# An attention-plus-MLP block on one core: key groups in the outer loop, all row sums kept on chip, first rows taken tile by tile

## The chip, the cores and the metric

The kernel runs on one core of one Trainium2 chip. The metric is the device time of one execution in microseconds (us); lower is better. TensorE (PE) multiplies matrices into PSUM, its weight loads have a row of their own (PEld); VectorE (DVE), ScalarE (ACT) and GpSimd (POOL) work on tiles of 128 partitions; SyncE (SP) and POOL issue most of the transfers (DMA). "SPq" in a profile is a transfer being issued by SP.

## What is computed

```
mod = (silu(c) @ w_mod) -> sa, ca, ga, sb, cb, gb          # six rows of 512
h = layernorm(x) * (1 + ca) + sa                           # x: 2048 rows x 512
q = h @ wq                                                 # 32 heads of 128; 8 key/value groups, 4 heads each
o = softmax(q k^T / sqrt(128)) v                           # 2048 keys per group
x = x + ga * (o @ wo)
h = layernorm(x) * (1 + cb) + sb
z = gelu(h @ w_in);  z1, z2 = halves of 896                # w_in: 512 x 1792
g = w_sp @ layernorm(z2) + b_sp                            # w_sp: 2048 x 2048, over rows
x = x + gb * ((z1 * g) @ w_out)
```

All inputs and the output are bf16.

## The kernel before, in words

**Tiles.** The 2048 rows are 16 tiles of 128, in four chunks of four tiles (512 rows). A *unit* is one row tile with one key group (four heads): 128 units. A unit has eight *slots*. In slot i, `qk` (L874) makes scores of two key tiles (two matmuls of 512 columns: 4 heads x 128 rows) into one of two PSUM buffers `s_ps` and ACT takes their exponentials into `pT` (L881, 128x1024). `pv` (L898) makes eight matmuls of 129 columns for the unit before: per head, `pT` as weights, values with a column of ones as the moving side, so the softmax sum comes out as column 129. Every fourth slot DVE divides (L909, L910) into `onorm`. After the last slot SP issues a DMA that transposes `onorm` into `oT` (L918), which `wo_proj` (L928) needs as weights; its result is added to the row tile's f32 sum `xacc` (L941), in the last group also scaled, added to `x_sb` and measured for the second layernorm (L946, L947, L673, L674).

**Order of the work.** Chunks are outermost: for each of the four chunks the eight groups are gone through, four units each. So keys `kT` (by a transposing DMA, L689, on SP), values, `wo` (L692, L694, on POOL) and `wq` (L700, on POOL) are loaded 32 times, 512 KB each, and six `xacc` buffers serve. The loop over iterations `it` lays out, slot by slot: `qk(it)`, `pv(it - 1)`, in slots 0 to 3 one matmul of the query projection of the coming group (`qproj`, L815, its copy L823), in slots 4 to 7 one matmul of `wo_proj(it - 2)`. The first layernorm of the next chunk (`ln1_norm` L779 with a transposing DMA L787, `ln1_mod` L795) and the second one (`ln2_norm` L961, DMA L969, `ln2_mod` L975) are hung into slots. The program's order is only a priority: a planner of the language may reorder each engine's instructions.

**Start.** SP issues `c`, four x tiles, the transposed keys of groups 0 and 1 (L689), the rest of x and the MLP's weights; ACT issues `w_mod`; POOL issues `wq`, values and `wo`. The layernorm of all four tiles of chunk 0, the modulation columns (`mod_columns`, L755) and the whole query projection of group 0 come before the first unit, and so do the rows `ga`, `gb` (L842). Then SP is given 32 transposing DMAs for the first half of `w_sp` (`load_wsp`, L649).

**End.** After the last unit come the softmax-sum check (L1030 to L1048, one matmul) and the MLP, in three parts: for each chunk the two halves of `z` (z2: L1065, GELU L1072, its statistics L1077, L1080 and layernorm L1099; z1 transposed: L1085, L1092), with 32 more transposing DMAs for the other half of `w_sp`; then for each 512 output rows seven sums over 16 row tiles (`g_ps`, L1113), the addition of `b_sp` and multiplication by z1 (L1121, L1124), and the projection `o2_ps` (L1134), which DVE finishes (L1142, L1144) and SP writes out (L1145). A branch at the end runs a slower general path when the check's flag is set; on this data it isn't.

`rstd_of` (L659 to L666) is four small POOL operations per layernorm.

Of the kernel before, what the change touches and what calls it, by code (L numbers as in the profile page):

```python
# [15 lines left out]
P = 128  # L16
# [559 lines left out]
def kernel(  # L576
# [39 lines left out]

    x_dram = A_x[0].rearrange("(t p) d -> p t d", p=P)
# [3 lines left out]
    v_dram = A_v_cache[0].rearrange("g (t p) d -> p g t d", p=P)  # L621
    wmod_dram = w_mod.rearrange("(dt p) n -> p dt n", p=P)
# [6 lines left out]
    flag = flagp.tile([1, 1], mybir.dt.int32, name="flag")  # L629
    res = fast.enter_context(tc.tile_pool(name="res", bufs=1))  # L630
    x_sb = res.tile([P, NT, D], BF16, name="x_sb")
# [8 lines left out]
    h2T = res.tile([P, NDT, S], BF16, name="h2T")  # L640
    win_sb = res.tile([P, NDT, F], BF16, name="win_sb")
    wout_sb = res.tile([P, NFT, D], BF16, name="wout_sb")
    bsp_bc = res.tile([P, S], BF16, name="bsp_bc")
    wsp = [None] * NCH
    nc.gpsimd.memset(mhalf[:], -0.5)

    def load_wsp(t):
        for st in range(NT):
            nc.sync.dma_start_transpose(  # L649
                out=wsp[t][:, st, :],  # L650
                in_=B_w_sp[t * 512 : (t + 1) * 512, st * P : (st + 1) * P],
            )

    stat = fast.enter_context(tc.tile_pool(name="stat", bufs=2))

    def rstd_of(mv, n, tag):

        ve = stat.tile([P, CT], FP32, name=f"ve_{tag}")
        nc.gpsimd.tensor_scalar(  # L659
            out=ve[:, :n], in0=mv[:, :, 1], scalar1=LN_EPS, scalar2=None, op0=ALU.add  # L660
        )
        rstd = stat.tile([P, CT], FP32, name=f"rstd_{tag}")
        nc.gpsimd.tensor_tensor(out=rstd[:, :n], in0=ve[:, :n], in1=mhalf[:, :n], op=ALU.pow)
        nmr = stat.tile([P, CT], FP32, name=f"nmr_{tag}")
        nc.gpsimd.tensor_tensor(out=nmr[:, :n], in0=mv[:, :, 0], in1=rstd[:, :n], op=ALU.mult)
        nc.gpsimd.tensor_scalar(  # L666
            out=nmr[:, :n], in0=nmr[:, :n], scalar1=-1.0, scalar2=None, op0=ALU.mult
        )
        return rstd, nmr
# [6 lines left out]
    with tc.tile_pool(name="psum", bufs=1, space=bass.MemoryType.PSUM) as psum, tc.tile_pool(  # L676
        name="kv", bufs=2
    ) as kvp, tc.tile_pool(name="wts", bufs=2) as wts, tc.tile_pool(
        name="acts", bufs=2
    ) as acts, tc.tile_pool(name="small", bufs=3) as small, tc.tile_pool(  # L680
        name="xacc", bufs=6
    ) as xaccp:
        groups = {}

        def load_group(n):

            g = n % HKV
            kT = kvp.tile([P, SK], BF16, name="kT")
            nc.sync.dma_start_transpose(out=kT[:], in_=A_k_cache[0, g])  # L689
            v1 = kvp.tile([P, NKT, DV], BF16, name="v1")  # L690
            nc.gpsimd.memset(v1[:, :, DH:DV], 1.0)  # L691
            nc.gpsimd.dma_start(out=v1[:, :, 0:DH], in_=v_dram[:, g])  # L692
            wo_g = wts.tile([P, REP, D], BF16, name="wo_g")
            nc.gpsimd.dma_start(out=wo_g[:], in_=wo_dram[:, g * REP : (g + 1) * REP, :])  # L694
            groups[n] = dict(kT=kT, v1=v1, wo=wo_g)

        def load_wq(n):
            g = n % HKV
            wq_g = wts.tile([P, NDT, REP * DH], BF16, name="wq_g")
            nc.gpsimd.dma_start(  # L700
                out=wq_g[:], in_=wq_dram[:, :, g * REP * DH : (g + 1) * REP * DH]
            )
            return wq_g

        wqs = {}
        hTs = {}
        qTs = {}

        with tc.tile_pool(name="setup", bufs=1, side="right") as setup:
            wmod_sb = setup.tile([P, NDT, NMOD], BF16, name="wmod_sb")  # L710
            c_bf = setup.tile([P, NDT], BF16, name="c_bf")
            nc.sync.dma_start(out=c_bf[:], in_=c_dram)
            for j in range(CT):
                nc.sync.dma_start(out=x_sb[:, j, :], in_=x_dram[:, j, :])
            nc.scalar.dma_start(out=wmod_sb[:, :, 0 : 2 * D], in_=wmod_dram[:, :, 0 : 2 * D])
            wqs[0] = load_wq(0)
            load_group(0)
            nc.scalar.dma_start(
                out=wmod_sb[:, :, 2 * D : NMOD], in_=wmod_dram[:, :, 2 * D : NMOD]
            )  # L720
            wqs[1] = load_wq(1)
            load_group(1)
            for t in range(1, NCH):
                nc.sync.dma_start(
                    out=x_sb[:, t * CT : (t + 1) * CT, :],
                    in_=x_dram[:, t * CT : (t + 1) * CT, :],
                )
            nc.sync.dma_start(out=win_sb[:], in_=win_dram)
            nc.sync.dma_start(out=wout_sb[:], in_=wout_dram)
            nc.sync.dma_start(out=bsp_bc[:], in_=B_b_sp.partition_broadcast(P))  # L730

            sc = setup.tile([P, NDT], FP32, name="sc")
# [94 lines left out]
            for hh in range(REP):  # L827
                for f in qproj(0, hh):
                    f()
# [354 lines left out]
```

## Time and profile before

| | |
|---|---|
| median of 3 runs | 1531.6 us (1531.58, 1531.60, 1538.72) |
| the profiled execution's own time | 1537.63 us |
| its span, first to last instruction | 1535.8 us |
| PE busy / ACT busy / DVE busy | 1348.6 / 1081.1 / 467.3 us |
| mean granted TensorE clock | 0.968 |
| DMA traffic | 108.99 MB, of which 58.85 MB read from HBM |

The profiled execution lies 1.8 us above its span and 6.0 us above the median. Busy times of PE overlap from one matmul to the next, so pace is read from start to start. In a row of a group stand line, engine, operation, tiles, count, then busy us and mean ns of one; in a timeline row start and length in us, and in brackets the idle time before it and who ended it; in a wait row the total, the number and the longest.

### The profile page before, as it was taken

The page shows a single profiled execution, that of the slowest core. Times are in us where ns is not written, and L with a number is a line of the kernel's source. Part 1 is how long each engine was busy: PE and PEld are TensorE (multiplying, and loading weights), DVE is VectorE, ACT ScalarE, POOL GpSimd, SP SyncE. Part 2 cuts the span into 40 slices and gives each one's busy share as a digit, 9 for nine tenths or more (in the row PEclk, how much of TensorE's full clock was granted, in tenths as well). Part 3 has the DMA queues.
Part 4 walks back from the last instruction along what each step waited for, and adds up shares of the span by engine and source line. Part 5 has one row for each costly group of instructions (what it writes and reads, how often), then busy time and mean ns, then how long its engine had stood idle before and what let it go on. Part 6 is the DMA issues. An engine that isn't in the chain of part 4 may idle for free.

```text
span 1535.8 us, 27625 instructions
## 1 busy us (share of the span) xinstructions
PE 1348.6 (88%) x11955; PEld 875.5 (57%) x12169; DVE 467.3 (30%) x1153; ACT 1081.1 (70%) x1087; POOL 123.7 (8%) x229
## 2 busy tenths in 40 slices
PE   0639999999989989998998999989999998879997
PEld 0326666666656666665666666656666666634443
DVE  2402222222622222224422222234222222364443
ACT  0428887888878878887888888878888888744000
POOL 2100000000200000001100000011100000010000
PEclk9969999999999999999999999999999999989999
DMA  9433333333333323324433323233333332132000
GB/s 300 114 76 70 70 70 66 70 70 70 87 79 70 69 60 72 73 57 80 86 70 70 69 62 70 61 72 80 70 70 70 70 56 39 23 71 53 15 21 23
DMA packets 210002, 108.99 MB, mean 71 GB/s; under 512 B 190928, under 2 KB 195920, under 8 KB 209872
## 3 DMA queue, kind: packets, MB, share of 16 engines
q1 hardware_dynamic: 194992, 53.64, 19.3%
q0 software_dynamic: 13824, 50.34, 12.0%
q10 hardware_dynamic: 1056, 3.15, 0.6%
q8 instruction: 97, 1.59, 0.4%
q14 instruction: 33, 0.27, 0.1%
HBM read 58.85 MB, written 2.10 MB: 40 GB/s over the span
## 4 chain that ended last, share of the span: by engine, by line
PE 66%; DMA 22%; DVE 5%; SPq 4%; issue 1%; ACT 1%; POOL 1%; DVEq 0%; POOLq 0%; ACTq 0%
PE s_ps L874 22%; PE o_ps L898 22%; DMA oT<-onorm 20%; PE misc L928 6%; PE g_ps L1113 6%; PE misc L815 3%; SPq L649 3%; DMA xnT<-xn 2%; PE z_ps L1065 2%; SPq L689 2%; PE z_ps L1085 2%; DVE xacc L941 1%; PE o_ps L1134 1%; DVE onorm L910 1%; DVE bnst L673 1%
## 5 line engine op out<-in xcount | busy, mean ns | idle before, releaser
L881 ACT ACTIVATE pT<-s_ps 128x1024 bf16<-128x1024 f32 x1024 | 1044.6, 1026 | 285.2 <-PE s_ps L874 214.8
L898 PEld LDWEIGHTS <-pT 128*128 128x128 bf16 x8192 | 570.0, 99 | 251.2 <-issue 15.8
L898 PE MATMUL o_ps<-v,pT 128*128 128x129 bf16 x8192 | 657.7, 223 | 0.1
L874 PE MATMUL s_ps<-qT,kT 128*128 128x512 bf16 x2048 | 620.9, 385 | 35.4 <-DMA oT<-onorm 23.8
L909 DVE RECIPROCAL rall<-o_ps 128x2 f32<-128x2 f32 x256 | 43.9, 171 | 857.7 <-PE o_ps L898 857.7
L874 PEld LDWEIGHTS <-kT 128*128 128x128 bf16 x2048 | 199.9, 98 | 124.3 <-issue 8.2
L928 PE MATMUL misc<-wo_g,oT 128*128 128x512 bf16 x406 | 159.4, 394 | 85.9 <-DMA oT<-onorm 85.4
L815 PE MATMUL misc<-hT,wq_g 128*128 128x512 bf16 x420 | 158.6, 386 | 13.3 <-DVE hT L795 13.2
L928 PEld LDWEIGHTS <-oT 128*128 128x128 bf16 x512 | 51.4, 101 | 120.1 <-DMA oT<-onorm 118.9
L910 DVE TENSOR_TENSOR onorm<-o_ps,rall 128x256 bf16<-128x256 f32 x256 | 106.2, 415 | 0.2
L1113 PE MATMUL g_ps<-wsp,z 128*128 128x512 bf16 x440 | 96.9, 379 | 0.4
L823 DVE CAST qT<-misc 128x512 bf16<-128x512 f32 x128 | 88.2, 689 | 9.6 <-PE misc L815 4.8
L941 DVE TENSOR_TENSOR xacc<-misc,xacc 128x512 f32<-128x512 f32 x112 | 77.3, 690 | 4.6
L1113 PEld LDWEIGHTS <-z 128*128 128x128 bf16 x448 | 43.8, 98 | 52.9
L815 PEld LDWEIGHTS <-wq_g 128*128 128x128 bf16 x512 | 50.9, 100 | 17.6 <-issue 17.2
L700 POOL DMA_DIRECT2D wq_g<-in_A_wq_dram x32 | 24.9, 777 | 376.8 <-PE misc L815 215.7
L694 POOL DMA_DIRECT2D wo_g<-in_A_wo_dram x32 | 24.6, 770 | 305.2 <-PE misc L928 198.6
L1121 DVE TENSOR_TENSOR gb<-g_ps,bsp_bc 128x512 bf16<-128x512 f32 x28 | 19.4, 692 | 65.2 <-PE g_ps L1113 65.2
L692 POOL DMA_DIRECT2D v<-in_A_v_cache_dram x32 | 37.5, 1172 | 6.5 <-issue 6.5
L755 PE MATMUL misc<-sc_bf,wmod_sb 128*128 128x1 bf16 x96 | 2.7, 164 | 35.9 <-DVE sc_bf L742 35.9
L691 POOL MEMSET v<- 128x32 bf16 x32 | 4.1, 128 | 358.1 <-issue 246.3
L673 DVE BATCH_NORM_STATS2 bnst<-x_sb 128x6 f32<-128x512 bf16 x32 | 21.7, 689 | 22.9 <-DMA x_sb<-in_A_x_dram 22.4
(61 smaller groups left out, 331.1 us busy)
## 6 DMA issues: line engine op xcount, KB each, us to landing
wq_g<-in_A_wq_dram POOLq DMA_DIRECT2D x32, 512.0 KB, 4.0
v<-in_A_v_cache_dram POOLq DMA_DIRECT2D x32, 512.0 KB, 6.8
wo_g<-in_A_wo_dram POOLq DMA_DIRECT2D x32, 512.0 KB, 4.7
wmod_sb<-in_w_mod_dram ACTq DMA_DIRECT2D x1, 2048.0 KB, 20.2
oT<-onorm SPq DMA_TRANSPOSE x128, 3.8
out_dram<-yout SPq DMA_DIRECT2D x16, 128.0 KB, 1.7
win_sb<-in_B_w_in_dram SPq DMA_DIRECT2D x1, 1792.0 KB, 11.2
x_sb<-in_A_x_dram SPq DMA_DIRECT2D x3, 512.0 KB, 6.2
```

The lines of the kernel that those rows point to most:

```text
L649: nc.sync.dma_start_transpose(out=wsp[t][:, st, :], in_=B_w_sp[t * 512 : (t + 1) * 512, st * P : (st + 1) * P],)
L692: nc.gpsimd.dma_start(out=v1[:, :, 0:DH], in_=v_dram[:, g])
L815: nc.tensor.matmul(q_ps[:], lhsT=wqs[n][:, dt, hh * DH : (hh + 1) * DH], rhs=hTs[ch][:, dt, :], start=(dt == 0), stop=(dt == NDT - 1),)
L823: nc.vector.tensor_copy(out=qTs[n][:, hh, :], in_=q_ps[:])
L874: nc.tensor.matmul(s_ps[:, h * 512 : (h + 1) * 512].rearrange("p (r q) -> p r q", r=REP), lhsT=groups[n]["kT"][:, kt * P : (kt + 1) * P], ...
L881: nc.scalar.activation(out=pTs[u][:, 2 * i : 2 * i + 2, :], in_=s_ps[:].rearrange("p (k q) -> p k q", k=2), func=ACT.Exp, scale=inv_sqrt_dh,)
L898: nc.tensor.matmul(o_ps[:, hh % 2, 0 : DH + 1], lhsT=pTs[u][:, kt, hh * P : (hh + 1) * P], rhs=groups[n]["v1"][:, kt, 0 : DH + 1], start=( ...
L909: nc.vector.reciprocal(out=rall[:, c0 : c0 + 2], in_=o_ps[:, :, DH])
L910: nc.vector.tensor_tensor(out=onorms[u][:, hh - 1 : hh + 1, :], in0=o_ps[:, :, 0:DH], in1=rall[:, c0 : c0 + 2].unsqueeze(2).to_broadcast([ ...
L928: nc.tensor.matmul(X_ps[:], lhsT=oTs[u][:, hh, :], rhs=groups[n]["wo"][:, hh, :], start=(hh == 0), stop=(hh == REP - 1),)
L941: nc.vector.tensor_tensor(out=xaccs[j][:], in0=X_ps[:], in1=xaccs[j][:], op=ALU.add)
L1113: nc.tensor.matmul(g_ps[:], lhsT=z2[:, st, f * P : (f + 1) * P], rhs=wsp[t][:, st, :], start=(st == 0), stop=(st == NT - 1),)
```

## The change

1. **Loops.** Groups are outermost: unit `u` is group `u // 16`, row tile `u % 16`. Each group's four loads are issued once (8 instead of 32 of each), in iterations 4 to 7 of the 16 of the group before. Sixteen `xacc` tiles hold all rows' sums, and all four chunks' `hT` stay in SBUF.
2. **Order.** A manual schedule fixes each engine's order to the program's.
3. **`wo_proj` one unit later**: `it - 3` in place of `it - 2`, three `oT` buffers.
4. **Start.** All loads go out on SP. Keys of group 0 come untransposed (row p of partition p, sixteen keys per partition; values likewise) and are turned by 16 PE transposes, copied by ACT. Row tile 0 is normalised and turned by PE alone, with its own query projection of 128 columns per head; tiles 1 to 3 are turned ahead of the first `qk`, and their projection (384 columns) fills the slots of iteration 0. The other chunks' layernorms stand in iterations 0, 2 and 5 with 16 PE transposes each; the columns for the second layernorm and the rows `ga`, `gb` in iteration 3. The first quarter of `w_sp` is loaded one transposing DMA every six iterations from iteration 21 on.
5. **Layernorm.** `rstd_of` has two POOL operations (add, power) instead of four; DVE subtracts the mean itself.
6. **MLP input beside the last units.** From iteration 128 on, three matmuls of `z` follow each slot (`zrun(3)`): z2 of tiles 0 to 11, then z1 of chunks 0 and 1; z2 of tiles 12 to 15 and z1 of chunks 2 and 3 follow. One GELU covers a whole z2 tile (896 columns) or two chunks of z1 (1024). `w_out` and `b_sp` are loaded then, on POOL; the second and third quarter of `w_sp` on SP after the loop, the fourth after the first quarter has been used.
7. **MLP output.** Each `o2` tile of a quarter is made between the sums of the next one. In the last quarter the sums are split into 384 and 128 columns, and the `o2` of the first three tiles runs beside them; the last tile is finished and written in two halves, by SP and ACT.

The core of the diff:

```diff
+    fast.enter_context(tc.manual_schedule())
+    nc.sync.dma_start(out=k_nat[:].rearrange("p (t d) -> p t d", d=DH), in_=k_rows[:, 0])
...
+    for kt in range(NKT):
+        nc.tensor.transpose(
+            k_ps[:, kt * P : (kt + 1) * P], k_nat[:, kt * P : (kt + 1) * P], ident[:]
+        )
...
-        units = [(n, jj) for n in range(NCH * HKV) for jj in range(CT)]
-        NU = len(units)
+    NU = HKV * NT
...
+    def qk(u, i):
+        g, j = divmod(u, NT)
+        b, jj = g * NCH + j // CT, j % CT
...
+                xaccs[j] = late.tile([P, D], FP32, name=f"xacc{j}", bufs=1)
...
+    rest0 = qproj(0, list(range(REP)), P, 512 - P)
+    at(0, 0, lambda: ln1_turn(1, CT - 1, xns0))
+    for i in range(NSLOT):
+        fill[0, i] = rest0[2 * i : 2 * i + 2]
+    ln1_at(0, 1)
+    ln1_at(2, 2)
+    ln1_at(5, 3)
+    at(3, 0, mod_rest)
...
+    for st in range(NT):
+        at(21 + 6 * st, 2, lambda st=st: load_wsp(wsp[0], 0, st))
+    for g in range(1, HKV):
+        it = (g - 1) * NT + 4
+        at(it, 3, lambda g=g: load_k(g))
+        at(it + 1, 3, lambda g=g: load_v(g, v_dram, nc.gpsimd))
+        at(it + 2, 3, lambda g=g: load_wo(g, nc.gpsimd))
+        at(it + 3, 3, lambda g=g: load_wq(g, nc.gpsimd))
...
+    for it in range(NU + 6):
...
-            wf = wo_proj(it - 2) if it >= 2 and it - 2 < NU else []
+        wf = wo_proj(it - 3) if 3 <= it < NU + 3 else []
+        for i in range(NSLOT):
+            for fn in later.pop((it, i), []):
+                fn()
             if it < NU:
+                qk(it, i)
+            if 1 <= it <= NU:
+                pv(it - 1, i)
+            for fn in fill.pop((it, i), []):
                 fn()
+            if i >= 4 and wf:
+                wf[i - 4]()
+            if it >= NU:
+                zrun(3)
```

`set_fill(b)` spreads the 16 matmuls of the next block's query projection over slots 0 to 3 of four iterations, as before; `at(it, slot, fn)` hangs a step into a slot.

## The prediction on record

> **What bounds the kernel now.** I read the page first, to see which engine sets the pace; then ACT's timeline, whose exponentials are the clockwork of the 128 units; then PE's waits inside the long stretch of units, and the granted clock by stage.
>
> ```profile
> span 1535.8 us, 27625 instructions
> PE 1348.6 (88%) x11955; PEld 875.5 (57%) x12169; DVE 467.3 (30%) x1153; ACT 1081.1 (70%) x1087; POOL 123.7 (8%) x229
> ...
> L881 ACT ACTIVATE pT<-s_ps 128x1024 bf16<-128x1024 f32 x1024 | 1044.6, 1026 | 285.2 <-PE s_ps L874 214.8
> ```
>
> PE is the fullest engine and ACT waits for it. The timeline gives the pace of both:
>
> ```profile
> 60.46 19.36 ACT L881 ACTIVATE pT<-s_ps 128x1024 bf16<-128x1024 f32 x21 [53.74 <-PE s_ps L874]
> 106.20 1.02 ACT L881 ACTIVATE pT<-s_ps 128x1024 bf16<-128x1024 f32 x1 [26.39 <-PE s_ps L874]
> ...
> 111.83 8.78 ACT L881 ACTIVATE pT<-s_ps 128x1024 bf16<-128x1024 f32 x8 [0.31 <-PE s_ps L874]
> ...
> 620.36 8.77 ACT L881 ACTIVATE pT<-s_ps 128x1024 bf16<-128x1024 f32 x8
> 629.28 8.77 ACT L881 ACTIVATE pT<-s_ps 128x1024 bf16<-128x1024 f32 x8
> ...
> 1328.60 7.91 ACT L881 ACTIVATE pT<-s_ps 128x1024 bf16<-128x1024 f32 x8
> ```
>
> Two unhindered units start 629.28 - 620.36 = 8.92 us apart: 1.115 us a slot. ACT alone could do a slot in (19.36 - 1.03) / 20 = 0.917 us, as its first 21 exponentials show. So an unhindered unit is PE's, and 8.92 us is its price. The units' real rate is worse: 24 exponentials lie ahead of 111.83, so unit 3 starts there, and unit 127 at 1328.60. That is 1216.8 us for 124 units, 9.81 each. Why:
>
> ```profile
> PE misc L928 <- DMA oT<-onorm: 54.5, 39, 4.2
> PE s_ps L874 <- DMA oT<-onorm: 23.8, 12, 3.0
> PE s_ps L874 <- ACT pT L881: 1.8, 5, 0.9
> ...
> 80.00:106.00 26.00, 1.30 (x4) 0.48 (x5) 0.00 (x0) 0.00 (x0) 0.00 (x0) 0.56 0.43 96
> 106.00:112.00 6.00, 5.78 (x41) 3.99 (x41) 0.83 (x3) 3.25 (x4) 0.00 (x0) 0.61 0.00 0
> 112.00:1328.00 1216.00, 1125.77 (x10701) 764.98 (x10893) 337.26 (x865) 1013.81 (x992) 98.38 (x167) 0.98 0.33 68
> 1337.00:1355.00 18.00, 5.49 (x57) 3.45 (x54) 13.73 (x37) 0.00 (x0) 3.92 (x12) 0.76 0.15 31
> 1355.00:1407.00 52.00, 51.31 (x242) 24.62 (x246) 29.66 (x70) 35.03 (x61) 6.81 (x16) 0.95 0.41 84
> 1407.00:1528.00 121.00, 120.14 (x546) 53.97 (x555) 52.26 (x87) 0.00 (x0) 0.00 (x0) 1.00 0.05 16
> ```
>
> The waits are PE's between 112 and 1328 us: 78.3 us on the transposed `oT`, next to nothing on ACT. The windows (columns: PE, PEld, DVE, ACT, POOL, clock, DMA share, GB/s) add that the granted clock is 0.98 there, some 0.02 x 1216 = 24 us more, and where it is below 1 PE had just stood idle (80 to 112, 1337 to 1355). [...] The 24 us are not added to the difference below, which holds them already.
>
> **The change part by part.** Six pieces of the span, each before and after.
>
> *First exponential.* The start before:
>
> ```profile
> 3.65 23.00 SPq L689 DMA_TRANSPOSE kT<-in_A_k_cache_dram  x2
> 6.31 0.17 DVE L734 CAST c_f<-c_bf 128x4 f32<-128x4 bf16 x1 [5.31 <-DMA c_bf<-in_c_dram]
> 32.13 1.29 DVE L673 BATCH_NORM_STATS2 bnst<-x_sb 128x6 f32<-128x512 bf16 x2 [9.91 <-DMA x_sb<-in_A_x_dram]
> 50.14 6.53 PE L815 MATMUL misc<-hT,wq_g 128*128 128x512 bf16 x16 [13.25 <-DVE hT L795]
> ...
> 60.07 42.06 SPq L649 DMA_TRANSPOSE wsp<-in_B_w_sp_dram  x32
> ...
> 0.00:40.00 40.00, 0.99 (x32) 1.03 (x33) 11.07 (x39) 1.49 (x2) 8.67 (x19) 1.00 0.97 302
> ...
> L673 DVE BATCH_NORM_STATS2 bnst<-x_sb 128x6 f32<-128x512 bf16 x32 | 21.7, 689 | 22.9 <-DMA x_sb<-in_A_x_dram 22.4
> L663 POOL TENSOR_TENSOR rstd_ln<-ve_ln,mhalf 128x4 f32<-128x4 f32 x4 | 4.1, 1029 | 9.5 <-DVE xn L779 9.5
> L961 DVE TENSOR_SCALAR xn<-x_sb,rstd_ln,nmr_ln 128x512 bf16<-128x512 bf16 x16 | 6.6, 413 | 24.3 <-POOL nmr_ln L666 24.3
> ```
>
> SP's 23 us on the transposed keys and DVE's wait for x go. Afterwards what the first `qk` needs ends with x tiles 1 to 3, behind `c`, tile 0, 1 MB of `w_mod` and 512 KB of keys: 2.05 MB, 6.8 us at the 302 GB/s of the first 40 us. Counted from the queue's start that is 8 us, from `c`'s landing near 6 it is 13; I take 10. Then three statistics (3 x 0.69, and 0.2 each for the aggregation, 2.7), POOL's power (1.03 and 0.5 around it), three `xn` (1.2), twelve PE transposes at half clock (no such row; by a 129-column `pv` matmul, 0.055 us warm, 0.11 cold, 1.4; by the cold 512-column one of L815, 0.41, it would be 4.9; the width decides for the first) and a `qk`, 0.6: first exponential near 18, with queueing among the small steps 20, between 17 and 27. Before 60.46: **-40.5**.
>
> *Units 0 to 2.* Before 111.83 - 60.46 = 51.4 us: PE stood 26.39 us for the first `oT`, queued behind 42 us of `w_sp` transposes on SP. Those are now one every six units. After: 8 slots at ACT's 0.917, two units at 8.92, 25.2; DVE has about 9 us of work in iteration 0 (the next chunk's four statistics and `xn`, 5.1, and eight PSUM copies at some half us, an estimate) against 7.3 us, and PE needs that `hT` next: +3 (0 to 6). **-23.2.**
>
> *Units 3 to 126.* The pace of a 512-column matmul is read from an undisturbed run of them, less the last one's 0.38:
>
> ```profile
> 1476.53 10.74 PE g_ps L1113 x49
> ```
>
> ```profile
> L910 DVE TENSOR_TENSOR onorm<-o_ps,rall 128x256 bf16<-128x256 f32 x256 | 106.2, 415 | 0.2
> ```
>
> so (10.74 - 0.38) / 48 = 0.216 us. Before 1216.8. After 120 units at 8.92 (1070.4), and four without projection (iterations 3, 124, 125, 126) at 8.92 - 4 x 0.216 = 8.06 (32.2): 1102.6, **-114.2** if the late `oT` is gone. Is it?
>
> ```profile
> DMA to landing us min/median/max: 2.4/3.8/8.1
> ```
>
> `onorm` is done some 0.6 us after the last `pv` slot (0.415 of it is the row above, the rest the reciprocal ahead of it); `wo_proj` needs `oT` in slot 4 of the next iteration but one of the `pv`: four slots and 0.9 us on, so 4.8 us against a median of 3.8 and a maximum of 8.1 from issue to landing. One unit more makes 13.7 us: covers the worst, with 5 us for SP's queue. What is next late is nothing in the row of PE's waits but ACT's 1.8 us. DVE's queue: `onorm`, the `qT` copy and `xacc` are the same per unit. SP's queue: behind each `load_k` stands an `oT` 4.5 us later, and one `w_sp` transpose comes every six units.
>
> Added on PE: 48 transposes of later tiles (0.055 each, 2.6), and `mod_rest`, which leaves the start: 32 one-column matmuls (0.99 in the 0:40 row) and eight of 512 columns (1.7). **+5.3.** Three of four group loads go, off the path; worth nothing by themselves.
>
> *Last exponential to the last z matmul.*
>
> ```profile
> 1355.64 8.33 PE z_ps L1065 x32
> ...
> 1370.01 6.05 PE z_ps L1065 x32
> ...
> 1406.30 4.96 PE g_ps L1113 x23
> ```
>
> Before: unit 127's exponentials end at 1336.5, the first z matmul starts at 1355.64 and cold (8.33 against 6.05), and the first row sum starts at 1406.30: 69.8 us. After: z itself, 128 x 6.05 / 32 = 24.2 and 112 x 0.216 = 24.2; 64 `pv` matmuls, 3.6; twelve of `wo`, 2.6: 54.6 of PE work without a gap. The cover of the layernorm chain is now z2 of tiles 0 to 11, and DVE becomes the narrow one:
>
> ```profile
> L1077 DVE BATCH_NORM_STATS2 stz<-z 128x6 f32<-128x448 bf16 x32 | 19.2, 611 | 9.9 <-ACT z L1072 8.3
> L1099 DVE TENSOR_SCALAR z<-z,rstd_lnz,nmr_lnz 128x896 bf16<-128x896 bf16 x16 | 7.1, 508 | 8.3 <-POOL nmr_lnz L666 8.3
> L975 DVE TENSOR_SCALAR h2T<-xnT,modc 128x128 bf16<-128x128 bf16 x64 | 16.7, 331 | 31.3 <-DMA xnT<-xn 31.3
> L674 DVE BATCH_NORM_AGGREGATE mv<-bnst 128x2 f32<-128x6 f32 x32 | 5.3, 176 | 0.5
> ```
>
> Until tile 15's `h2T`: twelve z2 statistics (twice 0.61 and an aggregation, 17), twelve z2 layernorms (6.1) and about 5 waiting for POOL's power, three row tiles finished by three passes and a statistics one of 0.69 and an aggregation (8.8), four `xn` (1.6), five `h2T` (6.6), the last unit's division (1.2): 46.5 us, while PE comes to z2 of tile 15 after some 41. Stall +3 (0 to 8). 57.6; **-12.2.**
>
> *Sums over rows and output.*
>
> ```profile
> 1358.64 43.09 SPq L649 DMA_TRANSPOSE wsp<-in_B_w_sp_dram  x32
> ...
> 1521.33 6.40 PE L1134 MATMUL o_ps<-wout_sb,yT 128*128 128x512 bf16 x27
> ...
> 1529.91 0.69 DVE L1144 TENSOR_TENSOR yout<-tmp,x_sb 128x512 bf16<-128x512 f32 x1 [1.44 <-DMA out_dram<-yout]
> ```
>
> 560 matmuls at 0.216 are 120.9 us of the 121.5 there; splitting columns 384 + 128 keeps their number of columns. Gain at most 0.6. The fourth quarter's 16 transposes (43.09 / 32 = 1.35 each, 21.6 us) now stand ahead of the first output transfers on SP; with two `yout` buffers DVE stands at the third tile from about 15 to 23 us into that quarter, and PE's two PSUM banks cover 8.5: +0 to 3, taken as 0.6. After the last matmul (1527.7) came 8.1 us; half tiles on two queues spare one pass, and the wait on `yout`: **-2.**
>
> *Sum.* 1535.8 - 40.5 - 23.2 - 114.2 + 5.3 - 12.2 - 2 = **1349** us of span, 1351 of device time. The profiled execution stood 6.0 above the median of the runs shown; I can't tell from which rows, and take off half: **1348**.
>
> **The rivals.** *The tail of queues is longer* (DVE in the z stage, SP in the output, start late): every bound at its upper end, 7 + 3 + 5 + 2.4, or one FIFO order that I misread, gives 1365 to 1388. For: DVE, 29.66 us busy in the 52 us of the old z stage, becomes nearly full, as the layernorms and sums of the last rows join it. Against: each piece has cover. 0.13.
>
> *`oT` stays late where loads share SP:* seven key loads, 16 `w_sp` transposes and sixteen layernorm ones, at 3 to 4 us with the clock's price: +75 to +155, 1425 to 1500. Against: 13.7 us of slack and 8.1 at worst. 0.04.
>
> *PE without pauses gets less clock; slower than before.* [...] The PE-bound part is 1102 + 55 + 121 = 1278 us; it decides below a clock of 0.87, where they grow by 184, and at the 0.76 of the 1337:1355 row they would grow by 404: 1752. Against: 1.00 in the 1407:1528 row, PE 120.14 of 121 us busy. 0.02. [...]
>
> *The fixed order puts a new wait into each unit.* `pv` needs the previous unit's last exponential in slot 1, whose end is at 620.36 + 8.77 = 629.13 in the rows above, while that `pv` follows a `qk` whose own exponential starts near 629.28 + 1.115 = 630.4: 1.2 us to spare. A wait of over 184 / 128 = 1.44 us in all units would make it slower than before. Against: the old slots show the same sequence and 1.8 us of such waits in all. 0.03 near 1550, a third of that within 0.5% of the old time.
>
> *It doesn't do what it says:* the extra unit of slack only pays if the planner had not already moved `wo_proj` as late; the waits of 78.3 us on `oT` show that it hadn't. Then only start and drain would gain, 1348 + 114 = 1462. 0.01 beside the case of the late `oT`.
>
> **How the numbers follow.** Forecast 0.77, with its own range 1332 to 1364 (start -3 to +7, DVE -3 to +5, units' first stage -3 to +3, the half of 6 us either way). The queue case reaches 1388; 1332 to 1388 holds some 0.88 by these chances, and I keep its width because one reading of a queue carries the upper part. Measurement tells about 0.5% (8 us). Faster 0.95, same 0.01, slower 0.04.
>
> **What would show it.** Right: first exponential at 17 to 27 us; unit starts 8.92 apart with hardly a wait on `oT`; clock at 1.00 from 25 us on; HBM reads down by 24 x 2 MB = 48 of 58.85 MB; no PE gap above 3 us before the sums; some waits of z2's matmuls on `h2T`. Wrong: PE waiting for `oT` near key loads; exponentials waited for in slot 1; DVE rows between last `pv` and z2 of tile 12 with PE idle above 8 us; a clock under 1 in the units.

## The result, and the profile after

| | us | ratio to before, 95% interval |
|---|---|---|
| before, median of 4 runs beside the changed kernel | 1533.41 (1531.58 to 1538.72) | 1 |
| the changed kernel, median of 4 runs | 1362.37 (1362.17 to 1363.74) | 0.8881 [0.8857, 0.8906] |
| forecast | 1348, range 1332 to 1388 | |

The time fell by 11.2% and lies in the range, 14.4 us above the forecast. The page of the changed kernel first: span, engines, traffic, and the group of exponentials that the prediction started from.

```profile
span 1360.8 us, 27642 instructions
PE 1318.9 (97%) x12137; PEld 873.7 (64%) x12345; DVE 476.7 (35%) x1171; ACT 1079.6 (79%) x1059; POOL 45.5 (3%) x88
...
HBM read 21.63 MB, written 2.10 MB: 17 GB/s over the span
...
L886 ACT ACTIVATE pT<-s_ps 128x1024 bf16<-128x1024 f32 x1024 | 1046.0, 1024 | 106.5 <-PE s_ps L879 30.3
```

PE's share went from 88% to 97%; ACT's exponentials cost what they did, but stand idle for 106.5 us instead of 285.2. ACT's timeline gives the stages:

```profile
17.11 1.02 ACT L886 ACTIVATE pT<-s_ps 128x1024 bf16<-128x1024 f32 x1 [4.60 <-PE s_ps L879]
...
28.50 8.83 ACT L886 ACTIVATE pT<-s_ps 128x1024 bf16<-128x1024 f32 x8 [0.70 <-PE s_ps L879]
...
51.87 7.91 ACT L886 ACTIVATE pT<-s_ps 128x1024 bf16<-128x1024 f32 x8 [3.46 <-PE s_ps L879]
59.93 8.77 ACT L886 ACTIVATE pT<-s_ps 128x1024 bf16<-128x1024 f32 x8 [0.15 <-PE s_ps L879]
68.85 7.66 ACT L886 ACTIVATE pT<-s_ps 128x1024 bf16<-128x1024 f32 x7
...
1157.09 7.91 ACT L886 ACTIVATE pT<-s_ps 128x1024 bf16<-128x1024 f32 x8
...
1198.60 1.94 ACT L1108 ACTIVATE z1T<-s_ps 128x1024 bf16<-128x1024 f32 x2 [8.53 <-DVE x_sb L952]
```

Units 4 and 5 start 68.85 - 59.93 = 8.92 us apart, the price of an unhindered unit in the prediction. Unit 3 starts at 51.87 and unit 127 at 1157.09. The last row does not belong to the units: it is the next to be read. PE's longest waits say the same from the other side:

```profile
PE o_ps L759 <- DMA wmod_a<-in_w_mod_dram: 7.3, 1, 7.3
PE s_ps L1100 <- ACT z1T L1108: 7.1, 1, 7.1
PE misc L796 <- DVE hT L803: 3.3, 3, 1.1
PE misc L1205 <- DVE gb L1214: 1.4, 1, 1.4
PE misc L796 <- DVE xn L679: 1.1, 1, 1.1
PE s_ps L1220 <- DVE tmp L1235: 1.1, 1, 1.1
```

No wait on `oT` is left. The first row lies in the start; the second is a wait that the kernel before did not have. By stage (PE, PEld, DVE, ACT, POOL, clock, DMA share, GB/s):

```profile
28.50:1157.10 1128.60, 1115.65 (x10960) 767.71 (x11147) 351.02 (x887) 1030.37 (x1009) 30.82 (x54) 1.00 0.16 32
1165.00:1229.30 64.30, 56.93 (x306) 28.55 (x309) 47.99 (x118) 29.16 (x31) 9.92 (x18) 0.92 0.32 74
1229.30:1353.60 124.30, 120.82 (x659) 60.93 (x670) 53.12 (x100) 1.02 (x1) 0.00 (x0) 1.00 0.20 47
```

In the units the clock is 1.00 and the DMA share half of the 0.33 before. It is the middle stage, the rest of `z`, that falls behind: PE is idle for 7.4 of its 64.3 us, at a clock of 0.92. The first row sum starts at 1229.13. So, between the same points of both traces (us):

| stage | before | after | difference | forecast |
|---|---|---|---|---|
| start to first exponential | 60.46 | 17.11 | -43.4 | -40.5 |
| to unit 3 | 51.4 | 34.8 | -16.6 | -18.7 |
| unit 3 to unit 127 | 1216.8 | 1105.2 | -111.6 | -113.3 |
| unit 127 to the first row sum | 77.7 | 72.0 | -5.7 | -12.2 |
| row sums to the end | 129.5 | 131.7 | +2.2 | -2 |
| span | 1535.8 | 1360.8 | -175.0 | -186.7 |

(The forecast's +5.3 is spread here as it falls: 0.9 each for the transposes of iterations 0, 2 and 5, 2.7 for the rows in iteration 3, ahead of unit 3.)

### The profile page after: what moved, and what is told of

It reads as the page before. It is cut to its first block, busy times and chain, and to the rows that moved or that the text cites. A ratio compares the mean times of both kernels' runs of the same rounds, so it can differ in the third digit from the quotient of the medians.

```text
span 1360.8 us, 27642 instructions
## 1 busy us (share of the span) xinstructions
PE 1318.9 (97%) x12137; PEld 873.7 (64%) x12345; DVE 476.7 (35%) x1171; ACT 1079.6 (79%) x1059; POOL 45.5 (3%) x88
## 3 DMA queue, kind: packets, MB, share of 16 engines
HBM read 21.63 MB, written 2.10 MB: 17 GB/s over the span
## 4 chain that ended last, share of the span: by engine, by line
PE 93%; DVE 3%; SPq 2%; issue 1%; DMA 1%; POOL 0%; ACT 0%; ACTq 0%; POOLq 0%; DVEq 0%
PE o_ps L901 35%; PE s_ps L879 35%; PE misc L843 7%; PE misc L933 6%; PE misc L1205 6%; PE s_ps L1100 2%; SPq L1012 1%; PE o_ps L1220 1%; PE s_ps L1064 1%; DMA wq_g<-in_A_wq_dram 1%; DVE stz L1081 1%; PE misc L796 0%; PE s_ps L1220 0%; DVE hT L803 0%; DVE z L679 0%
## 5 line engine op out<-in xcount | busy, mean ns | idle before, releaser
L886 ACT ACTIVATE pT<-s_ps 128x1024 bf16<-128x1024 f32 x1024 | 1046.0, 1024 | 106.5 <-PE s_ps L879 30.3
L843 PE MATMUL misc<-hT,wq_g 128*128 128x512 bf16 (+2 forms) x462 | 169.1, 376 | 0.8 <-DMA wq_g<-in_A_wq_dram 0.8
L933 PE MATMUL misc<-wo_g,oT 128*128 128x512 bf16 x386 | 145.7, 377 | 0.0
L1205 PE MATMUL misc<-wsp,z 128*128 128x512 bf16 (+2 forms) x555 | 100.5, 336 | 1.9 <-DVE gb L1214 1.4
L852 DVE CAST qT<-misc 128x512 bf16<-128x512 f32 (+1 forms) x129 | 87.3, 676 | 1.7 <-PE misc L843 1.7
L1214 DVE TENSOR_TENSOR gb<-misc,bsp_bc 128x512 bf16<-128x512 f32 (+2 forms) x35 | 20.4, 584 | 60.9 <-PE misc L1205 60.9
L1100 PE MATMUL s_ps<-hT,win_sb 128*128 128x512 bf16 x109 | 27.2, 408 | 7.3 <-ACT z1T L1108 7.1
L1108 ACT ACTIVATE z1T<-s_ps 128x1024 bf16<-128x1024 f32 x14 | 14.2, 1024 | 20.1 <-PE s_ps L1100 11.6
L1064 PE MATMUL s_ps<-win_sb,hT 128*128 128x448 bf16 x128 | 27.0, 352 | 0.1
L1074 ACT ACTIVATE z<-s_ps 128x896 bf16<-128x896 f32 x16 | 14.7, 917 | 15.0 <-PE s_ps L1064 15.0
L1100 PEld LDWEIGHTS <-win_sb 128*128 128x128 bf16 x112 | 11.6, 103 | 22.5 <-issue 11.0
## 6 DMA issues: line engine op xcount, KB each, us to landing
win_sb<-in_B_w_in_dram SPq DMA_DIRECT2D x1, 1792.0 KB, 13.7
```

Source lines behind the costliest of these rows:

```text
L843: nc.tensor.matmul(ps[0][:, o0 : o0 + n], lhsT=wqs[g][:, dt, hh * DH : (hh + 1) * DH], rhs=hTs[ch][:, dt, c0 : c0 + n], start=(dt == 0), s ...
L852: nc.vector.tensor_copy(out=qTs[b][:, hs[0] : hs[-1] + 1, c0 : c0 + n], in_=ps[0][:, 0 : len(hs) * n].rearrange("p (h q) -> p h q", q=n),)
L886: nc.scalar.activation(out=pTs[u][:, 2 * i : 2 * i + 2, :], in_=s_ps[:].rearrange("p (k q) -> p k q", k=2), func=ACT.Exp, scale=inv_sqrt_dh,)
L933: nc.tensor.matmul(X_ps[:], lhsT=oTs[u][:, hh, :], rhs=groups[g]["wo"][:, hh, :], start=(hh == 0), stop=(hh == REP - 1),)
L1064: nc.tensor.matmul(ps[0][:, hf * 512 : hf * 512 + FC], lhsT=h2Ts[j // CT][:, dt, (j % CT) * P : (j % CT + 1) * P], rhs=win_sb[:, dt, FH + ...
L1100: nc.tensor.matmul(ps[0][:, k * 512 : (k + 1) * 512], lhsT=win_sb[:, dt, f * P : (f + 1) * P], rhs=h2Ts[2 * ch2 + k][:, dt, :], start=(dt ...
```

## The experiments

Eleven kernels, in three batches, each with runs of the kernel before on the same chip (medians 1536.1, 1535.9 and 1534.8). None leaves out work. Times are compared with the changed kernel's 1362.37 directly where the difference is well above the spread of the runs.

**Is it the unit of slack, or the traffic that is gone?** The largest term, the late `oT`, has two possible causes for its end: `wo_proj` stands one unit later (theory A), or three quarters of the loads no longer stand beside the transfers (rival B). Two kernels do one without the other.

*The old loop order with only `wo_proj` (and the second layernorm) one unit later:*

```diff
-        for it in range(NU + 3):
+        for it in range(NU + 4):
...
-            if it >= 2 and it - 2 < NU:
-                wn, wjj = units[it - 2]
+            if it >= 3 and it - 3 < NU:
+                wn, wjj = units[it - 3]
...
-            wf = wo_proj(it - 2) if it >= 2 and it - 2 < NU else []
+            wf = wo_proj(it - 3) if it >= 3 and it - 3 < NU else []
```

> The kernel before with one edit: wo_proj and the second layernorm behind it take unit it - 3 in place of it - 2, so oT has 13.7 us instead of 4.8 us before PE needs it. Theory A (the slack is what the 114 us between units 3 and 126 were short of): the waits of PE on oT between 112 and 1328 us fall from 78 us to under 15, units start 8.9 to 9.1 us apart there, the time falls by 90 to 115 us to 1420 to 1445. Rival B (oT is late because SP and the 16 DMA engines are full of the 32-fold group loads, and lateness just grows with the queue): the waits stay above 45 us and the time falls by less than 40 us.

Measured 1428.44 us (1427.79 to 1430.97), ratio 0.9294 [0.9253, 0.9336]. PE's waits, without those ahead of the first unit:

```profile
PE misc L928 <- DMA oT<-onorm: 22.6, 2, 18.7
...
PE f_ps L1047 <- DVE bad L1041: 11.4, 1, 11.4
PE o_ps L898 <- DVE onorm L910: 6.2, 5, 2.8
```

What `oT` takes from issue to landing, in the view of that tile, and then the stage of the units in the windows:

```profile
DMA to landing us min/median/max: 2.4/4.0/8.1
```

```profile
112.00:1217.00 1105.00, 1098.81 (x10810) 748.29 (x10808) 334.53 (x859) 1004.73 (x984) 97.14 (x166) 1.00 0.37 74
```

Of what is left on `oT`, 18.7 us lie at the start, behind the `w_sp` transposes, and 3.9 behind the last unit; between 112 and 1217 us PE is busy for 1098.8 of 1105.0. Landing is as slow as it was (median 4.0, maximum 8.1; 3.8 and 8.1 before), so nothing arrives earlier: it is only asked for later. Theory A holds: one unit of slack, in four lines, is worth 1536.1 - 1428.4 = 107.7 us by itself, of 171.0 for the whole change.

*The new kernel with `wo_proj` at its old distance* (from iteration 9 on; iteration 8 does two units):

```diff
-        wf = wo_proj(it - 3) if 3 <= it < NU + 3 else []
+        if it < 8:
+            wf = wo_proj(it - 3) if it >= 3 else []
+        elif it == 8:
+            wf = wo_proj(5) + wo_proj(6)
+        else:
+            wf = wo_proj(it - 2) if it < NU + 2 else []
```

> The changed kernel with wo_proj at it - 2 again (from unit 7 on; units 5 and 6 share iteration 8, the layernorm behind it moves with it). Theory A (slack alone took the waits away): with 4.8 us oT is late again, 60 to 110 us more, 1420 to 1470. Rival B (traffic alone): oT now lands in a median of 2.4 us instead of 3.8, which fits into 4.8; only the ones next to the seven key loads, the 16 w_sp transposes and the last layernorms are late, some 30 times up to 3 us: 0 to 30 us more, 1360 to 1392. If e1 falls as A says and this one stays as B says, either of the two changes would have done alone.

Measured 1369.80 us (1368.97 to 1371.72), ratio 0.8917 [0.8877, 0.8957]. PE's first wait, the landing of `oT`, and ACT's unit 127:

```profile
PE misc L933 <- DMA oT<-onorm: 14.4, 13, 2.0
```

```profile
DMA to landing us min/median/max: 2.4/2.4/6.8
```

```profile
1174.18 7.91 ACT L886 ACTIVATE pT<-s_ps 128x1024 bf16<-128x1024 f32 x8 [0.15 <-PE s_ps L879]
```

Landing has a median of 2.4 us with the loads gone, and 13 waits of at most 2.0 us are all that comes back. Unit 127 starts 17.1 us later than in the changed kernel; as the last sums come one unit earlier and the 7.1 us wait on `z1T` is gone, some 10 are given back and 7.4 remain. So rival B holds as well: the new order with its fewer loads, at the old distance, leaves 14.4 of the old 78.3 us of waits; the slack alone leaves none from unit 4 to the last. The two are not additive; the change pays twice for most of this term. Which part of the new order does it is not separated here: besides the group loads that are gone, SP no longer has the burst of `w_sp` transposes ahead of the units, nor the transposing DMAs of the first layernorm.

**What is the new 7 us wait?** After the units DVE ends a row sum late, ACT's first z1 GELU waits for it, and PE for ACT, though z1 has no use for the second layernorm of tile 15. The timelines of DVE, then PE, of the changed kernel:

```profile
1194.53 1.78 DVE L679 TENSOR_SCALAR z<-z,mvz,rstd_lnz 128x896 bf16<-128x896 bf16 x4 [1.48 <-POOL rstd_lnz L675]
1196.23 0.69 DVE L946 TENSOR_TENSOR xacc<-misc,xacc 128x512 f32<-128x512 f32 x1
...
1197.67 0.69 DVE L952 TENSOR_TENSOR x_sb<-xacc,x_sb 128x512 bf16<-128x512 f32 x1
...
1199.67 11.48 PE L1100 MATMUL s_ps<-hT,win_sb 128*128 128x512 bf16 x39 [7.11 <-ACT z1T L1108]
```

ACT starts at 1198.60, 0.24 us after L952 has ended. L952 is the last reader of the row sums `xacc`, and `z1T` is laid into the memory that their pool leaves (theory A); DVE is late there because z2 layernorms and their wait for POOL stand ahead of it. The rival is that ACT or PE itself was late.

*z2's first three layernorms after the last row sums:*

```diff
-            zq[-1] = [zq[-1], lambda ch=j // CT: z2_norm(ch)]
+            pass
...
+    for ch in range(3):
+        z2_norm(ch)
```

> The changed kernel with the layernorms of z2 of chunks 0 to 2 issued after the last z1 tile of chunks 0 and 1 instead of between the z2 tiles: the same work, later in DVE's queue. Theory A (ACT's first z1 GELU waits 8.5 us for the last row sum on DVE because z1T lies in the memory that the row sums leave, and DVE gets there late since two rounds of z2 layernorms of 1.8 us and their 1.5 us waits for POOL stand ahead): DVE comes there some 6.5 us earlier, PE's 7.1 us stall on s_ps falls below 1.5 us, the time falls by 5 to 7 us to 1355 to 1358. Rival B (DVE's sum of work is the bound): the same work only moves, PE waits for h2T at tiles 12 to 15 or the row sums wait for z2, and the time stays within 2 us.

Measured 1353.29 us (1353.11 to 1353.44), ratio 0.8807 [0.8768, 0.8846], 9.1 us less than the changed kernel. DVE's and ACT's timeline, PE's wait, and the stage's window:

```profile
1190.94 0.69 DVE L952 TENSOR_TENSOR x_sb<-xacc,x_sb 128x512 bf16<-128x512 f32 x1
...
1191.87 1.94 ACT L1108 ACTIVATE z1T<-s_ps 128x1024 bf16<-128x1024 f32 x2 [1.90 <-DVE x_sb L952]
```

```profile
PE s_ps L1100 <- ACT z1T L1108: 0.5, 1, 0.5
```

```profile
1165.00:1220.00 55.00, 54.52 (x310) 27.97 (x309) 47.19 (x117) 29.15 (x31) 11.38 (x18) 1.00 0.34 81
```

The row sum ends 6.7 us earlier, ACT follows it as before, and PE's wait is 0.5. The gain is larger than the wait, as the clock of that stage goes from 0.92 to 1.00 too. PE's 54.5 us between 1165 and 1220 are the "54.6 us of PE work without a gap" of the prediction.

*The first half of the first three z1 tiles in memory beside z2 instead:*

```diff
+            zs["z1a"] = z2p.tile([P, 3, 1024], BF16, name="z1a")
...
-            zs["z1T"] = mlp.tile([P, NFT, S], BF16, name="z1T")
+            zs["z1b"] = mlp.tile([P, NFT - 3, 1024], BF16, name="z1b")
+            zs["z1c"] = mlp.tile([P, NFT, 1024], BF16, name="z1c")
```

> The changed kernel, DVE's order untouched, but the first half of the first three z1 tiles lies in memory beside z2 and not in that of the row sums; the other four z1 tiles stay where they were. Theory A (the 7.1 us stall is a wait for memory: ACT's first GELU of z1 waits until DVE has used the last row sum, nothing in the data asks for it): three GELUs go ahead, PE's wait on s_ps falls from 7.1 to 1 to 3 us, the time falls by 4 to 6 us to 1356 to 1358. Rival B (DVE's amount of work bounds the stage, the memory only names the place): PE stands as long a few tiles later, on h2T or on the sums' z2, the time stays within 2 us of 1362.

Measured 1356.73 us (1356.50 to 1356.94), ratio 0.8832 [0.8797, 0.8866]. ACT's timeline, then PE's waits:

```profile
1191.17 1.02 ACT L1113 ACTIVATE z1a<-s_ps 128x1024 bf16<-128x1024 f32 x1 [0.81 <-PE s_ps L1105]
...
1198.90 1.94 ACT L1113 ACTIVATE z1b<-s_ps 128x1024 bf16<-128x1024 f32 x2 [3.25 <-DVE x_sb L952]
```

```profile
PE s_ps L1105 <- ACT z1b L1113: 1.9, 1, 1.9
...
PE s_ps L1064 <- DVE hT L977: 1.3, 1, 1.3
```

DVE's order is as in the changed kernel, yet the tiles in their own memory are written 7.4 us sooner; the first that lies in the row sums' memory, `z1b`, still waits for L952. That shows the memory as the cause. The last row is the wait on the second layernorm's columns that the prediction had named for this place. In the changed kernel it doesn't show; with the planner, below, it stands beside the other one.

**Does the fixed order matter?**

*The changed kernel with the planner:*

```diff
-    fast.enter_context(tc.manual_schedule())
```

> The changed kernel without the manual schedule, so that the planner orders each engine again. Theory A (the fixed order is worth nothing in the units, whose slots look the same before and after, and a little at start and end): units still 8.92 us apart, the time within -5 and +15 us of 1362. Rival B (the planner's order was part of the lost 114 us): waits of over 30 us on oT or on exponentials appear, 1395 or more.

Measured 1371.17 us (1370.02 to 1372.59), ratio 0.8926 [0.8887, 0.8966]. PE's waits (line numbers are one lower here), then ACT's unit 127:

```profile
PE s_ps L1099 <- ACT z1T L1107: 8.1, 1, 8.1
...
PE s_ps L1063 <- DVE hT L976: 4.0, 1, 4.0
```

```profile
1157.53 7.91 ACT L885 ACTIVATE pT<-s_ps 128x1024 bf16<-128x1024 f32 x8 [0.15 <-PE s_ps L878]
```

Unit 127 starts 0.4 us later than with the fixed order: the units gain nothing by it. Almost all of the 8.8 us comes after that, where DVE is narrow. The start holds a lesson of its own: here the first exponential came at 22.79 us, 5.7 later than in the changed kernel, and yet unit 3 started at 52.18, only 0.3 later. An early first exponential is worth little by itself as long as PE has the same work to do up to unit 3.

*The old loop order with later `wo_proj`, and the `w_sp` transposes spread* (written into iterations 8, 11, 14 and so on, in place of one burst ahead of the units):

```diff
-            load_wsp(t)
...
+        for k in range(2 * NT):
+            at(8 + 3 * k, 2, lambda k=k: nc.sync.dma_start_transpose(
+                out=wsp[k // NT][:, k % NT, :],
...
```

> The kernel of e1 (before with the later wo_proj), and the 32 w_sp transposes that SP issued in one go ahead of the first units now one every three iterations from iteration 8 on. Theory A (the first units stand for oT behind that burst alone): the 18.7 us wait of e1 goes, unit 4 starts some 19 to 24 us sooner than its 112.0 us, the time falls from 1428 to 1404 to 1410, and no new wait on oT appears. Rival B (the first units wait for something else as well, the burst only shows): unit 4 starts less than 10 us sooner, 1418 or more.

Measured 1427.72 us (1425.02 to 1431.47), ratio 0.9288 [0.9251, 0.9325]: no change. SP's timeline says why, and PE's wait on `oT` is the old one:

```profile
60.11 42.10 SPq L989 DMA_TRANSPOSE wsp<-in_B_w_sp_dram  x31
```

```profile
PE misc L926 <- DMA oT<-onorm: 21.4, 2, 17.5
```

The planner issued 31 of the 32 at once, as soon as SP was free. The run tells nothing about the burst; it shows that written order is only a priority there.

*The same with the fixed order:*

```diff
+    fast.enter_context(tc.manual_schedule())
```

> The kernel of e5 with a manual schedule, so that each engine keeps the program's order; e5 had shown that the planner pulls the w_sp transposes back to the front (31 of the 32 issued from 60 to 102 us again), so the burst was never moved. Theory A (the burst is what the first units wait for; moving it takes a fixed order): the 17.5 us wait of PE on oT goes, unit 4 starts near 95 us or earlier instead of 112, the time falls from 1428 to 1400 to 1412. Rival B (the start is slow for another reason, or the program's order makes new waits in the old loop): 1420 or more.

Measured 1415.75 us (1415.49 to 1416.39), ratio 0.9231 [0.9195, 0.9266]. ACT's timeline, then one of PE's waits:

```profile
57.33 32.16 ACT L880 ACTIVATE pT<-s_ps 128x1024 bf16<-128x1024 f32 x32 [50.70 <-PE s_ps L873]
89.64 8.77 ACT L880 ACTIVATE pT<-s_ps 128x1024 bf16<-128x1024 f32 x8 [0.15 <-PE s_ps L873]
```

```profile
PE f_ps L1051 <- DVE ones_c L1049: 15.7, 1, 15.7
```

Now the transposes are spread, and the first 32 exponentials run through: unit 4 starts at 89.64, 22.4 us earlier than the 112.01 of the kernel with only the later `wo_proj`. 2.7 of these are an earlier first exponential (57.33 instead of 60.04); the other 19.7 are the stall behind the burst. Theory A holds for the stall, but the time lies between the two ranges, as only 12 to 13 us reach the median: 3.2 are lost in the units, where PE now waits 8.1 us for `wq_g`, and 3.7 behind them, where it waits 15.7 us for the flag's matmul instead of 11.4; and the profile that is compared with lies 2.5 above its kernel's median. So the fixed order is what makes spreading possible, and it must be written right at every place.

*The changed kernel with the 16 transposes of the first quarter of `w_sp` in one burst, in iteration 21:*

```diff
-        at(21 + 6 * st, 2, lambda st=st: load_wsp(wsp[0], 0, st))
+        at(21, 2, lambda st=st: load_wsp(wsp[0], 0, st))
```

> The changed kernel with the 16 transposes of the first w_sp quarter issued together in iteration 21 instead of one every six iterations: 16 x 1.31 = 21 us of SP. Theory A (oT has 13.7 us and lands in 2.4, so a burst costs only what goes beyond 11.3 us): the oT behind it comes some 10 us late, one stall of 7 to 12 us with 1 to 2 us for the clock, 1370 to 1376. Rival B (the transfers themselves are too little to matter, SP's queue lets oT through): within 3 us of 1362.

Measured 1368.31 us (1366.89 to 1369.81), ratio 0.8907 [0.8872, 0.8943], 5.9 us more. The timeline of SP and of ACT, PE's wait, and the window around it:

```profile
215.10 22.35 SPq L1012 DMA_TRANSPOSE wsp<-in_B_w_sp_dram  x16
...
241.82 1.02 ACT L886 ACTIVATE pT<-s_ps 128x1024 bf16<-128x1024 f32 x1 [4.69 <-PE s_ps L879]
243.97 1.02 ACT L886 ACTIVATE pT<-s_ps 128x1024 bf16<-128x1024 f32 x1 [1.12 <-PE s_ps L879]
```

```profile
PE misc L933 <- DMA oT<-onorm: 4.2, 1, 4.2
```

```profile
241.00:246.00 5.00, 5.00 (x35) 3.31 (x34) 0.10 (x1) 2.62 (x3) 0.00 (x0) 0.66 0.12 22
```

SP issues for 22.35 us without a break, an `oT` stands behind it, and the unit of slack covers all but 4.2 us. Then two exponentials start 2.15 us apart instead of 1.115, at a clock of 0.66: the rest of the 5.9. The mechanism is the expected one, but the time lies between the two ranges: the `oT` that PE waited for became ready at 222.70, 7.6 us into the burst, and was issued at 237.96. Of these 15.3 us the slack of 11.3 covers all but 4.0; the expectation had it ready when the burst began.

**The start and the tail.**

*Keys of group 0 by a transposing DMA, at the same place of SP's queue:*

```diff
-    nc.sync.dma_start(out=k_nat[:].rearrange("p (t d) -> p t d", d=DH), in_=k_rows[:, 0])
+    nc.sync.dma_start_transpose(out=kT0[:], in_=A_k_cache[0, 0])
...
-    for kt in range(NKT):
-        nc.tensor.transpose(
...
```

> The changed kernel with the keys of group 0 loaded by one transposing DMA, as before, in the place of the plain load (no PE transposes, no ACT copies, keys and values of group 0 in their usual order). Theory A (the transposing load is slow while the start's loads fill the DMA engines: 18 us of issue in the trace before, and SP issues x tiles 1 to 3 behind it): first exponential at 28 to 37 us instead of 17.1, the time 11 to 20 us longer, 1373 to 1382. Rival B (in a queue of its own place it lands as it does in the units, 4.4 us after issue): first exponential before 21 us, 1359 to 1366.

Measured 1363.52 us (1363.16 to 1364.23), ratio 0.8890 [0.8856, 0.8925]. SP's and ACT's timeline:

```profile
2.25 4.74 SPq L699 DMA_TRANSPOSE kT<-in_A_k_cache_dram  x1
...
18.27 1.02 ACT L875 ACTIVATE pT<-s_ps 128x1024 bf16<-128x1024 f32 x1 [14.32 <-PE s_ps L868]
```

The transposing load keeps SP for 4.74 us here, and the first exponential comes 1.2 us later. In the kernel before, the first of the two such loads took 18.33 us and the second 4.62; together they are the 23.00 us (start, length):

```profile
3.65 18.33 SPq L689
22.03 4.62 SPq L689
```

My theory, that the transposing load is what held the start, falls; the rival holds.

*The last quarter's sums not split into 384 and 128 columns:*

```diff
-        spatial(last, yT, f, 0, n_a)
+        spatial(last, yT, f, 0, 512)
...
-    for f in range(NFT):
-        spatial(last, yT, f, n_a, P)
...
```

> The changed kernel with the last quarter's sums in 512 columns as in the other quarters, o2 of all four last tiles beside them and finished one after the other at the end. Theory A (the split pays by keeping DVE's finishing of three tiles off the end): the end grows by three tiles of 1.4 us, less the 1.7 us that PE waits inside the split part: 1363 to 1366. Rival B (the split only costs: short matmuls and DVE's extra small passes): 1358 to 1361.

Measured 1363.15 us (1362.89 to 1363.50), ratio 0.8887 [0.8853, 0.8921]. The 0.8 us are within the spread of the changed kernel's own runs (1362.17 to 1363.74): undecided, and at most worth a microsecond.

**A version that beats both.** The kernel with the later z2 layernorms, and besides: the layernorm of the early iterations one slot earlier with its two halves of transposes in two slots, and all outputs issued by ACT, away from SP's transposes.

```diff
-        at(it, 5, lambda: st.update(x=ln1_norm(ch * CT, CT, st["r"])))
-        at(it, 7, lambda: ln1_turn(ch * CT, CT, st["x"]))
+        at(it, 4, lambda: st.update(x=ln1_norm(ch * CT, CT, st["r"])))
+        at(it, 6, lambda: ln1_turn(ch * CT, CT, st["x"], (0,)))
+        at(it, 7, lambda: ln1_turn(ch * CT, CT, st["x"], (1,)))
...
-            (nc.sync if k == 0 else nc.scalar).dma_start(out=out_dram[:, j, s], in_=yout[:, s])
+            nc.scalar.dma_start(out=out_dram[:, j, s], in_=yout[:, s])
```

> The kernel of e3 and two more edits: the 16 PE transposes of each later chunk are laid into two slots (eight each, the layernorm one slot earlier), and all output transfers are issued by ACT, so that they don't stand behind the 16 transposes of the last w_sp quarter. Theory A: PE no longer waits 3.3 us for hT between the halves, DVE no longer stands 7.8 us for an output transfer and PE's 1.4 us there goes: 1353.3 falls by 4 to 6 us to 1347 to 1350. Rival B (these waits are covered by the next matmuls' slack or ACT's queue adds as much): 1352 or more.

Measured 1350.86 us (1350.84 to 1351.69), ratio 0.8795 [0.8761, 0.8830]: the fastest of all, 11.5 us under the changed kernel and 2.4 under the one with only the later layernorms. The two extra edits give less than expected: unit 127 starts at 1155.59 instead of 1156.99 (1.4 us, PE's wait on `hT` is 0.3 instead of 3.3, but 1.8 on `xn`), and 0.9 to 1.0 at the end, where the wait on `gb` is gone.

## Why the prediction was right, and where it was not

**First exponential: size right, one reason wrong.** Forecast at 20, measured 17.11. Of what I let go, "SP's 23 us on the transposed keys" was misread: the experiment with a transposing load has 4.74 us on SP and loses 1.2. The second of the two loads in the kernel before had cost no more (4.62); the 18.33 of the first were not the price of its kind: in the changed kernel's start a plain load of x (L731) holds SP for 6.29 us. What held the first so long is not shown. The twelve PE transposes, put at 1.4 us at half clock, took 1.69 to the `qk` behind them (14.32 to 16.01); two score matmuls took 1.06 us there and 0.59 from 21.37 on, though the granted clock is 1.00 from 14.32 to 20.40. What of the 43 us is due to the order on one queue, to the one tile that goes ahead, and to the projection moved into the slots, no run separates. Part of it is only moved: the run with the planner shows that a first exponential 5.7 us later leaves unit 3 where it is, so this term and the next are better read together, 60.0 us less where 59.2 were forecast.

**Units 0 to 2: 2.1 us too good.** Unit 0 took 28.50 - 17.11 = 11.4 us where 10.3 and 0.9 for the transposes were forecast. The two after it took 23.4 instead of 21.4: I counted the transposes but not that PE waits 1.1 us for the copy of their first half each time, nor the 0.6 us that it waits for the left side of the rows' matmuls (`lhs_bc`); those eight matmuls took 1.9 instead of 1.7. The PSUM copies of iteration 0, estimated at half a us, took 0.50 to 0.56.

**Units 3 to 126: right.** Price 8.92, no wait on `oT`, clock 1.00. The reason, slack over the worst landing, is shown by the experiment with slack alone, which has the same late landings and, from unit 4 on, no wait on `oT` in the units. That the new order with its smaller traffic would have done most of it by itself I had not said: the 13.7 us against 8.1 were compared as if landing stayed what it was, and its median fell from 3.8 to 2.4.

**Last exponential to the first row sum: the step that failed.** Forecast -12.2, measured -5.7. PE's work (54.6) and the narrow engine (DVE) were right; "Stall +3 (0 to 8)" had its place wrong. I followed the data of z2's last tiles to `h2T`, and the wait came through memory: `z1T` can't be written before the last row sum has been read, whatever z1 needs. It costs 7.1 us and, by the run with later layernorms, some 2 to 3 more in clock, which is 0.50 from 1199.6 to 1205.0 us. So the stage lost 64.1 - 54.6 = 9.5 us where I had put 3, at most 8: the wait alone lay inside that range, by luck, and the clock was not in it. Of the signs that I had set, "no PE gap above 3 us before the sums" failed, and no wait on `h2T` showed.

**Row sums to the end: 4.2 us too good.** The timeline of DVE and PE in the second quarter's sums:

```profile
1276.91 0.69 DVE L1236 TENSOR_TENSOR yout<-tmp,x_sb 128x512 bf16<-128x512 f32 x1 [7.82 <-DMA out_dram<-yout]
...
1278.26 10.52 PE L1205 MATMUL misc<-wsp,z 128*128 128x512 bf16 x48 [1.38 <-DVE gb L1214]
```

DVE stood 7.82 us on an output queued behind SP's transposes, as forecast, and PE paid 1.38 (0.6 forecast). The rest are small waits in the split last quarter, 1.1 on `tmp` and 0.6 on `yT`, which I put at nothing. From the first sum to the last matmul PE took 125.3 us where it had taken 121.4; with the 1.38 these waits are 3.1 of the 3.9, and 0.8 has no name. The tail after the last matmul did get shorter: 1360.8 - 1354.4 = 6.4 us against 8.1.

**From span to median: wrong way.** I took off 3 us for a profile that stood above the median of the runs shown. In the later batches the kernel before had medians of 1534.8 to 1536.1, and the changed kernel's profiled span of 1360.8 stands 1.6 under its median: only the 2 us around the span were real. The terms above make 11.7 of the 14.4 us, this one the rest.

**HBM reads.** They fell by 37.2 MB, not 48. The fourth load, the transposing one, is not in that line of the page: the plain loads that the DMA views list add up to all of it, 57473 KB or 58.85 MB before and 21121 KB or 21.63 MB after (1 KB is 1024 bytes), without one transposing load. Three kinds of 24 loads are 24 x 3 x 0.524 = 37.7 MB, and less the 0.5 of the plain key load that came in, 37.2.

**The rivals.** Longer queue tails came true in part, in the z stage and the output, inside the range. `oT` didn't stay late, the clock of the dense stage didn't fall (1.00 over 1128.6 us with PE busy 1115.65), and the fixed order put no wait into the units; without it they run the same.

## What to carry to other kernels

A transfer that an engine waits for a little in every round was cured here by a consumer one round later (no wait on `oT` from unit 4 to the last), and nearly by the loop order with fewer loads (14.4 of 78.3 us left); find out which is cheaper before doing both, since four lines gave 108 of the 171 us here. When matmuls are moved next to the end of another stage, follow not only the data but also the memory that the new tiles are laid into: the wait is then named after a step with which the waiting one has nothing to do. And a load's time on its queue can belong to the moment and not to its kind: the transposing load of one group's keys took 18.33 and then 4.62 us in one start.

## What the runs showed of the hardware

**After some waits of PE its granted clock was about half for a while, and those waits need not be long.** In the run with the burst, after PE's single wait of 4.2 us, two exponentials started 2.15 us apart instead of 1.115, and the clock was 0.66 from 241 to 246 us. In the changed kernel, after the wait of 7.1 us, it was 0.50 from 1199.6 to 1205.0. With `wo_proj` at its old distance, with 13 waits on `oT` of at most 2.0 us, the mean clock of the span was 0.999. In the kernel before PE's longest wait between 112 and 400 us was 2.9, and yet the clock fell several times there: to 0.50 from 214 to 216 us after a wait of 2.28, to 0.57 from 254 to 258 after that of 2.9, and here after a single wait on `oT` of 2.14 us, to 0.50 from 370.3 to 373.3:

```profile
365.00:370.00 5.00, 2.86 (x29) 1.85 (x28) 1.19 (x3) 2.41 (x4) 0.00 (x0) 1.00 0.63 107
370.00:375.00 5.00, 4.95 (x36) 3.12 (x35) 0.65 (x2) 3.03 (x3) 0.21 (x1) 0.66 0.00 0
```

Other waits of that size left the clock at 1.00: after 2.27 us without a PE matmul before 331.19 it was 1.00 from 330 to 335. So on this kernel the clock was lower after some waits of little over 2 us and not after others; what tells the two kinds apart is not shown.

**The same transposing transfer takes different times.** `oT` lands in a median of 4.0 us with a DMA share of 0.37 beside it (the old order with the later `wo_proj`), and in 2.4 with 0.16 (the changed kernel). That the traffic beside it makes the difference is read from these two kernels, not isolated. The 512 KB key load took SP 4.74 us in the experiment above, and 18.33 and 4.62 us for the two in the kernel before.
